# Attention and a sticky mixture of experts on one core: another written order for the same instructions

## The chip, the cores and the metric

The kernel runs on one core of a Trainium2 chip. The metric is device time in microseconds (us) of one execution, the median of several. The core has five instruction streams: TensorE (PE; its weight loads are listed as PEld), VectorE (DVE), ScalarE (ACT), GpSimd (POOL) and SyncE (SP), which here only issues DMAs. Each stream is worked off in the order in which the program issues it; streams wait for each other through semaphores.

## What is computed

First, causal attention with a decay on 8 batches of 8 heads, 576 positions and 64 values a head; its result, read as x of shape (8, 576, 512), goes through 8 experts. A position takes the expert of the position before it unless a local gate opens.

```python
scores = scale * q @ k.T + cum[:, None] - cum[None, :]      # cum = cumsum(log(clip(f)))
scores = where(causal, -1e9, scores); attn = softmax(scores)
x = (attn @ v)                                              # (B, S, H*D)
logits = x @ w_gate; local = sigmoid(x @ w_local)
for b, s:                                                   # in order of s
    fresh = argmax(logits[b, s])
    e = fresh if s == 0 or local[b, s] < 0.5 else prev_e
    out[b, s] = softmax(logits[b, s])[e] * (relu(x[b, s] @ w1[e]) @ w2[e])
```

## The kernel before

The program has two stages, one after the other: attention of all batches, up to about 369 us, and the experts, up to the end. Fp32 values are carried as pairs of fp16 numbers (a high and a low half), so a product is three matmuls.

**Attention.** A batch consists of 24 score units and a last one that needs no scores of its own. A unit runs through parts, each on one engine, and each part has a letter: S the scores on PE (L785, L792) into one of four PSUM banks `st`; M the maximum on DVE (L796) and N its joining (L890); E the exponential on ACT (L816); T four turns on PE (L830) into one of two banks `pt`; H the high half on ACT (L835); L the low half on DVE (L839), or in some units U on PE (L842) and K on ACT (L847) in its place; A the product with v on PE (L810). R and W divide (L861, L865 on DVE).

**What a batch needs.** q and k are loaded (L193, L197), split into halves by POOL (L317 to L327) into `t16q` and `t16k`, turned by DMA transposes from SP's queue (L362, into `Aq` and `Ak`; q and k are letters), and copied in part by further DMAs from the same queue into `QB` and `KB` (L370, L374; u and y). Scores read all four, in halves of four heads. `Aq` and `Ak` have two buffers each, `t16q` and `t16k` one. The result x is split by POOL (L317, L318), stored (L677), turned by DMA (L673 into `xt`, L701 into `xlt`; x and j) and multiplied with the gate's weights on PE (L735; g). Every second batch ends a group of tokens, for which steps of the routing follow (r): DVE finds the sticky choice, `G` (L1138 to L1148), PE turns it (L1153), and so on.

**What sets the order.** No scheduler: `ORDER` (L45) is a string of these letters, 2,244 of them, and `issue()` (L1042) walks it, issues the part that a letter names, for the oldest unit or step that has one left, and stops at the next S. `THEN` (L71) is a second string, of 314 letters, for the first part of the experts' stage: each letter asks one of 15 streams for its next piece (L1930), b products of early gathered tokens (L1809), c and d hidden values, e and f outputs (L1822), g the routing of the last group (L1901, L735, L1268 and on), h its probabilities, i the first expert's weights (L1620, L1607), j and k further weights, l and m gathered tokens, n ranks. So a letter's place in a string is the place of its instructions in the queues of the engines, SP's among them. z0 to z3 in `ORDER` (0, 1, 2, 3) are products of the first gathered tokens (L1533, hidden values L1539 and L1542) at attention's end.

Of the kernel before, what the change touches and what calls it, by code (L numbers as in the profile page):

```python
# [44 lines left out]
ORDER = (  # L45
    "SSMSMddMEddSTEMSHSdLTEMAHdSLTEMAHSMETLESHMSELTAEMSHMTSEMALHdSRELTWSHMTEALHSUREWTKMSHMdTEMAAHLtTEtLAcMHAcLRTSTW"
    "AHtEHUMEtKRtELTTcHAccttWHScUMALcSSETMMKEESTttHMHccAAyuuuULKANTSSERRTWWMbSMHNHLLE."
    "NAATTMHNHSLyLAAAEETTHbRbMSSWRbHWLSLbpETTMifiSAAAMHHLMTEEALAvMtHiSvELERMTTcHHLiLESfAWSMTiTiMASSHAHLLTpEEATHHMMx"
    "ASpUpElSKRELRWWTTMbMHLHEpSESATppyHMASSMEELTLAppAHTMEsAUSqpMHRWRUKKSqEpMbMTTHSHWAEELLAATTHSUMMHSKLEMpAEvRTTpHAH"
    "pNkUKuSsWRSLTTEAMMNHHWSE."  # L50
    "pNpLpATlLyHMASTEHAANSLxMpbTRREjSELpMbbTppHHWLEpfSMLEMpAASSTTHHkbbAMELWLAAiMETTygSSRWHHLLiiAAgEiiMMyuTuTfHHgLAL"
    "SSlTEEvTvMpAHiMSHlLSppRELAMTpEMTWRWpHSpHUKSEEpLATMAMxTxSSHEjAALEMMvTHHALSEERRWWTqUMgSgsKgSTpMppAHHLSLArEEMTTSr"
    "HHpUAMrLMEAuKrRETTrNpSpkrsrrHHAULETrMKWSTRNrEpWSHrMrAAAHLNMLEyTA."
    "HNRSrqLkppTEArppMHrbbTWSSLRTAHMLETMHbErLAHSSTLrTpEppWMHHrrbAAyLiLArMSpEfTTMRiiASrSirirHHuELLWbEMMTxTuHHAArrpES"
    "pSLTELbHTSMMALMpEvvAirTRRHySExHUSfKrlWSELTAHprWpMMAArSvsEETLTpMHHlpAAMSSLRRLMjrEpqTTESrSHWrLEprpTWMHHAALpEMMAk"
    "rUppAKSspTAMTuERHLHSWTLEESMTMppgggARHNSrpHyNLbbqWTLbkESTpEAHpMAAMNLrNEH."
    "ATLpHRESLpTTHHSSRWWLMMTALiiiEEfppMruAAAHSLTSApSHMEMLEETTAiiHbRHSSMWiELLTTMMfSSHHAyrALTrLEAErTlSMAMHpHrRLLMpEES"
    "THTpHSrUSRWAKTEHWrMLbrlrMLprErrrAESMrrbATxyrrMxpSrvHAjERETSrLMrHMqARrgrTUESHSKWLuTTggMMSEbrMHHruUvppAWEELrrppS"
    "KrrTpMSHMArTLAAENpHpksAyTLRETvrHHksRbWWSSApLNTAqLyrbMpTErHbMHNLAApN."
    "rpTEHSELrLprrubMRrfupTSTHHWArrLRALMESSErTHMMEEpTpWbvpLSiArTSSiiMMiiHHrrALLAATpEMTESSAHHrRLLrvWrsrTTfMMEHLHAALE"  # L60
    "EASSMrTTRMHESAErppLTRirHSvWUHMrLWrSKMMATAAlTAESpprHpEHLrTELpHMSTAsSyrRMEWRSHrpppLUrEWSTpbMMKTHHxxpLSAMMlApAEEk"
    "rrrTAUpqESKRHTLjSAHTMEMHULNKRSNWWMTppprTAyAHLHEAENEruSkArLqTT."
    "gpMrbbbrNHHrgEARLWLTpgArRHLTppSSTfrWrHMMrrLSSEHSLMMETTSEiAAApiipMrrHHMLLEASRTuuEHMiiTWHiLSLMrASrlETTASAAMEHHLp"
    "pELRTMETrrHAHWrrrySELvLSfvxTSHySMMRETEblLxMrWprAMHLESErSTpprrjbsHqMvMEASAATrHpLrMrTAHRRUSKLMSEETWpgMgHgSEMTUpp"
    "HKApprpSWETrpppALHTAArpHMpSkErLpNALTRETMWurSSHNRHrLELyW."
    "ArTrHMrTMAANrHNAUERKLErSTSrHWTHrMrEMSrELrLArkTSTrMAHsqAyrRLrSMrEHppAEASLTTHMMSWSrEEALMHRTiriLrSTEiAHHMurLELeeT"
    "HrMeeSMTEiiiWSSeeMLErelAAAMuTSeSsHHLURrMKrAWRTrMExHTWEAlAeeeerLHjrLSETSeerATHAEMLMHRALeTSsSxHTWeeAEErHUUKKyeeT"
    "TeRSSMrHHWAeeAMrLTEreLH01Mre2METAHLRrA3rRTEErWSeLWrrHUTKAAHMLNSMAhEATTHHeeRggNWzSLgLSMMNAeETEANER0123H00T1Wrhz"
    "2sH1r230L130LeThhTzzHHA1232L03e0hsh12e.13z2hALAA3zzRhWz"
)  # L70
# [2106 lines left out]
```

## Time and profile before

| | us |
|---|---|
| median of 3 runs | 768.9 (767.83 to 770.14) |
| the profiled execution | 768.85 |
| its span | 766.8 |
| PE busy | 716.1 (93%) |
| DVE, ACT, POOL busy | 478.0, 416.1, 409.9 |
| mean granted clock of TensorE | 0.985 |

The span is the stretch of the profiled execution between its first and last instruction; 2.05 us lie around it. Batches begin on PE at 15.4, 59.3, 95.8, 140.2, 180.2, 224.3, 269.9 and 310.2 us; the last score unit at 354.8. They are called batch 0 to 7.

### The profile page before, as it was taken

To read this page: it belongs to the slowest core of one execution; us is meant where nothing else is said; L and a number is where in the kernel's file an instruction comes from. 1 tells how busy PE (TensorE), PEld (TensorE's weight loads), DVE (VectorE), ACT (ScalarE), POOL (GpSimd) and SP (SyncE) were. 2 spreads that over 40 slices of the span, in tenths; PEclk is the share of its full clock that TensorE was granted. 3 is DMA by queue.
4 is the path that set the end of the run, shared out by engine and by line. 5 is a ranking of instruction groups with operands and counts; after the bars stand their busy time and mean duration, and the time that the engine had idled before them with its cause. 6 is when DMAs were issued, how large, how long until landed. Compare 5 with 4: busy or idle time off the path is not lost. (4 is left out here: it accounts for less than half of the span.)

```text
span 766.8 us, 20737 instructions
## 1 busy us (share of the span) xinstructions
PE 716.1 (93%) x8400; PEld 507.9 (66%) x8400; DVE 478.0 (62%) x1055; ACT 416.1 (54%) x795; POOL 409.9 (53%) x515
## 2 busy tenths in 40 slices
...
GB/s 197 224 160 234 199 229 207 215 204 235 202 219 283 185 228 199 211 231 110 204 265 105 257 40 230 148 231 81 185 180 90 240 103 198 175 125 167 44 7 46
DMA packets 181251, 136.07 MB, mean 177 GB/s; under 512 B 143971, under 2 KB 151397, under 8 KB 181111
## 3 DMA queue, kind: packets, MB, share of 16 engines
...
## 5 line engine op out<-in xcount | busy, mean ns | idle before, releaser
L816 ACT ACTIVATE P<-st,nm 128x512 f32<-128x512 f32 (+3 forms) x288 | 144.0, 561 | 14.5 <-DVE nm L890 7.5
L1442 PE MATMUL z<-xT,wh 128*128 128x300 f16 (+7 forms) x832 | 144.6, 289 | 0.3 <-DVE hl L1429 0.3
L796 DVE TENSOR_REDUCE nm<-st 128x1 f32<-128x512 f32 (+4 forms) x264 | 133.5, 542 | 9.5 <-PE st L792 6.9
L835 ACT CAST ph<-pt 128x512 f16<-128x512 f32 (+1 forms) x200 | 113.1, 587 | 36.9 <-PE pt L830 34.9
L830 PE MATMUL pt<-ident,P 128*128 128x128 f32 x784 | 117.7, 281 | 8.2 <-DVE pl L839 3.2
L839 DVE TENSOR_TENSOR pl<-pt,ph 128x512 f16<-128x512 f32 (+1 forms) x171 | 111.9, 667 | 11.9 <-ACT ph L835 11.1
L1434 POOL DMA_INDIRECT out_dram<-o,ranki x23 | 24.2, 1050 | 158.4 <-ACT o L1433 142.1
L1429 DVE SCALAR_TENSOR_TENSOR hl<-z,hh 128x240 f16<-128x240 f32 (+7 forms) x64 | 42.4, 662 | 96.2 <-ACT hh L1428 94.6
L1469 PE MATMUL y<-ul,hh 128*128 128x512 f16 (+2 forms) x440 | 101.1, 309 | 0.9 <-issue 0.9
L1469 PE MATMUL y<-uh,hh 128*128 128x512 f16 (+2 forms) x440 | 101.5, 311 | 0.1
L1469 PE MATMUL y<-uh,hl 128*128 128x512 f16 (+2 forms) x440 | 101.1, 309 | 0.1
L830 PEld LDWEIGHTS pt<-ident,P 128*128 128x128 f32 x784 | 84.6, 142 | 21.2 <-DVE pl L839 6.4
L1442 PEld LDWEIGHTS <-wh 128*128 128x128 f16 x832 | 80.8, 97 | 26.5 <-issue 0.7
L1442 PE MATMUL z<-xT,wl 128*128 128x300 f16 (+7 forms) x416 | 94.4, 289 | 0.0
L1469 PEld LDWEIGHTS <-hh 128*128 128x128 f16 (+2 forms) x880 | 56.9, 100 | 54.0 <-issue 6.1
L810 PE MATMUL xp<-VH,pl 128*128 128x65 f16 (+1 forms) x960 | 88.8, 195 | 2.6 <-DVE pl L839 2.3
L810 PE MATMUL xp<-VH,ph 128*128 128x65 f16 (+1 forms) x960 | 89.7, 196 | 0.0
L810 PE MATMUL xp<-VL,ph 128*128 128x65 f16 (+1 forms) x960 | 89.3, 195 | 0.3 <-issue 0.3
L810 PEld LDWEIGHTS <-ph 128*128 128x128 f16 (+1 forms) x1920 | 82.6, 103 | 7.5 <-issue 4.0
L1428 ACT ACTIVATE hh<-z 128x240 f16<-128x240 f32 (+7 forms) x64 | 36.7, 574 | 91.7 <-PE z L1442 88.3
L785 PE MATMUL st<-KB,QB 70*128 70x512 f16 (+5 forms) x384 | 77.2, 300 | 9.6 <-DMA KB<-Ak 6.9
L785 PE MATMUL st<-Ak,Aq 128*128 128x512 f16 (+5 forms) x384 | 77.1, 303 | 0.8 <-DVE nm L890 0.3
...
## 6 DMA issues: line engine op xcount, KB each, us to landing
...
```

Of the source, the lines that this page charges most:

```text
L785: nc.tensor.matmul(st[p0:p0 + m, co:co + n], lhsT=queries(lq, kk, h, c), rhs=rhs, start=(ps == 0 and first and co == col), stop=(ps == 1), ...
L796: nc.vector.tensor_reduce(dst, src, axis=AX.X, op=ALU.max, negate=True)
L810: nc.tensor.matmul(xo, lhsT=a[:, c0:c0 + m], rhs=w[:, vi, :], start=False, stop=(i == n - 1 and jj == 2), skip_group_check=True)
L816: nc.scalar.activation(P[:, c0:c1], st[:, c0:c1], AF.Exp, bias=bias)
L830: nc.tensor.matmul(U["pt"][:, i * 128:(i + 1) * 128], lhsT=P[:, i * 128:(i + 1) * 128], rhs=ident, is_transpose=True, start=(i == 0), stop ...
L835: nc.scalar.copy(U["ph"][:, :cols], U["pt"][:, :cols])
L839: nc.vector.tensor_tensor(U["pl"][:, :cols], U["pt"][:, :cols], U["ph"][:, :cols], ALU.subtract)
L1428: nc.scalar.activation(hv, z[:, 0:nh, 0:wd], AF.Relu)
L1429: nc.vector.scalar_tensor_tensor(lv, z[:, 0:nh, 0:wd], 0.0, hv, ALU.max, ALU.subtract)
L1434: nc.gpsimd.indirect_dma_start(out=outf, out_offset=bass.IndirectOffsetOnAxis(ap=scat(t), axis=0), in_=o, in_offset=None, bounds_check=NT ...
L1442: nc.tensor.matmul(z[:, a, 0:wd], lhsT=w[:, d, fc * 128:(fc + 1) * 128], rhs=xT[:, x, a * wd:(a + 1) * wd], start=(i == 0), stop=(i == len ...
L1469: nc.tensor.matmul(y[m * r:m * r + m, 0:w], lhsT=a[:, fc, c0:c0 + m], rhs=u[:, fc, w * r:w * r + w], start=(i == 0), stop=(i == len(prods) ...
```

## The change

Two string constants hold other permutations of the same letters; every letter occurs as often as before, and no function, buffer or shape differs. Lines keep their numbers. The diff is the two strings and nothing else; a line of each:

```diff
 ORDER = (
-    "SSMSMddMEddSTEMSHSdLTEMAHdSLTEMAHSMETLESHMSELTAEMSHMTSEMALHdSRELTWSHMTEALHSUREWTKMSHMdTEMAAHLtTEtLAcMHAcLRTSTW"
...
+    "SSMSMddMEddSTEMSHSdLTEMAHdSLTEMAHSMETLESHMSELTAEMSHMTSEMALHdSRELTWSHMTEALHSUREWTKMSHMdTEMAAHLtTEtLAcMHAcLRTAHt"
...
 THEN = (
-    "gggbbgbhhhbbbggbbbbbihbbgbbbcjgghjbbgbhhhhhgghbgbhhbhbbibbgdhjhbjjjbhhhiibhbbhbigbggbbggkkbbbbgghgjbbbbgebggbb"
...
+    "hggbbbbghbghhhhihhbbbbbhhhhgghbbbbhbgjhhhhgbbbjbbbbbbhghbbbggigbhgbbigbbiiggghbbbbjjgggebbkjcgbbgggbdbbbgbgcgg"
...
```

The first line of `ORDER` is the same up to its last few letters. Behind them the units' parts, the DMAs and POOL's splits interleave in another way, batch by batch. Three places follow.

**PE, end of batch 2**, where the first group's sticky choice `G` is turned (L1153). Before:

```order
L785 MATMUL st<-KB_122,QB_120 64x512
L785 LDWEIGHTS QB_120
L785 MATMUL st<-KB_122,QB_120 64x512
L1153 LDWEIGHTS kp
L1153 MATMUL st<-ident_72,kp 128x128
L1153 LDWEIGHTS G
L1153 MATMUL st<-ident_72,G 128x128
```

After:

```order
L785 LDWEIGHTS QB_120
L785 MATMUL st<-KB_122,QB_120 64x512
L842 LDWEIGHTS minus
L842 MATMUL pt<-ph,minus 128x512
L830 MATMUL pt<-ident,P 128x128 x4
L1153 LDWEIGHTS kp
L1153 MATMUL st<-ident_72,kp 128x128
L1153 LDWEIGHTS G
L1153 MATMUL st<-ident_72,G 128x128
```

A second set of scores (one more unit), a subtraction (L842) and four turns (L830) now stand between the step that makes `G` and its turn.

**SP, batch 5, the second half of its heads** (the forms with 128x20x128 are the turns of heads 4 to 7 and the last chunk; QB1 and KB1 are the buffers that this batch's scores read). Before:

```order
L362 DMA_TRANSPOSE Ak_5174<-t16k_5173 128x20x128
L677 DMA xs_60<-xr_4452 128x2x1024
L193 DMA ldq_5151<-in_q_dram 128x1024
L362 DMA_TRANSPOSE Aq_4502<-t16q_4501 128x20x128
L370 DMA KB1_123<-Ak_5174 64x2048
L197 DMA ldq_5151<-in_q_dram 128x256
L193 DMA ldk_5421<-in_k_dram 128x1024
L370 DMA QB1_121<-Aq_4502 64x2048
L193 DMA ldk_5421<-in_k_dram 128x1024
L374 DMA QB1_121<-Aq_4502 64x512
```

After:

```order
L362 DMA_TRANSPOSE Aq_4305<-t16q_4304 128x20x128
L677 DMA xs_60<-xr_4407 128x2x1024
L193 DMA ldk_5433<-in_k_dram 128x1024
L370 DMA QB1_121<-Aq_4305 64x2048
L374 DMA QB1_121<-Aq_4305 64x512
L343 DMA QB0_120<-augm_61 3x4096
L352 DMA QB0_120<-augt_62 3x512
L362 DMA_TRANSPOSE Ak_4796<-t16k_4795 128x20x128
L193 DMA ldk_5433<-in_k_dram 128x1024
L197 DMA ldk_5433<-in_k_dram 128x256
L370 DMA KB1_123<-Ak_4796 64x2048
```

The two turns changed places, and both of q's copies now stand between them; k's copy comes last.

**POOL, attention's end** (x of batch 7 is split by L317 and L318; L1407 gathers tokens; L1381, L324 and L327 prepare weights; L696 clears `xlt` ahead of its last multiplication with the gate's weights). Before:

```order
L317 TENSOR_SCALAR xr<-xn 128x2x512
L318 TENSOR_TENSOR xr<-xn,xr 128x2x512
L317 TENSOR_SCALAR xr<-xn 128x512
L318 TENSOR_TENSOR xr<-xn,xr 128x512
L1381 TENSOR_SCALAR stg<-stg 128x1024
L1407 DMA xg<-xs,xg 128x1024 x4
L324 TENSOR_SCALAR uh<-stg 128x1024
L327 TENSOR_TENSOR ul<-stg,uh 128x512 x2
L696 MEMSET xlt 128x64
```

After:

```order
L317 TENSOR_SCALAR xr<-xn 128x2x512
L318 TENSOR_TENSOR xr<-xn,xr 128x2x512
L317 TENSOR_SCALAR xr<-xn 128x512
L318 TENSOR_TENSOR xr<-xn,xr 128x512
L1407 DMA xg<-xs,xg 128x1024 x4
L1381 TENSOR_SCALAR stg<-stg 128x1024
L324 TENSOR_SCALAR uh<-stg 128x1024
L327 TENSOR_TENSOR ul<-stg,uh 128x512 x2
L696 MEMSET xlt 128x64
```

The weights' scaling (L1381) went from ahead of the four gathers to behind them. On PE, the turn of the last x (L1901) was followed at once by the gate's multiplication (L735); now sixteen matmuls of the early products (L1809) stand between them, and four groups of three matmuls of L1533, before one, stand ahead of L1901 behind attention's last A.

## Rows read from the trace of the kernel before

**Rows 1.** Windows: start:end length, busy us (instructions) by engine, granted clock, DMA share, GB/s.
```profile
60.00:400.00 340.00, 310.98 (x5053) 249.39 (x5050) 299.55 (x729) 254.30 (x542) 265.80 (x304) 0.97 0.96 215
...
360.00:400.00 40.00, 33.45 (x378) 24.23 (x377) 25.89 (x67) 11.24 (x22) 18.97 (x17) 0.87 0.81 234
400.00:766.00 366.00, 358.20 (x2772) 223.50 (x2770) 131.35 (x237) 116.07 (x166) 87.94 (x121) 1.00 0.51 140
```
The engines' columns are PE, PEld, DVE, ACT, POOL, in this order.

**Rows 2.** Windows of the three stretches at half clock.
```profile
133.40:140.20 6.80, 6.80 (x70) 4.65 (x69) 4.26 (x13) 3.61 (x8) 6.46 (x7) 0.50 0.89 190
...
198.20:201.60 3.40, 3.40 (x28) 3.02 (x27) 2.40 (x8) 0.44 (x1) 1.13 (x1) 0.50 1.24 135
...
372.30:382.50 10.20, 7.73 (x103) 7.64 (x100) 3.77 (x24) 1.06 (x4) 4.17 (x5) 0.50 0.70 170
```
**Rows 3.** Waits of PE: line, what for; us in total, times, longest us.
```profile
PE st L785 <- DMA KB<-Ak: 6.9, 4, 2.1
...
PE st L785 <- DMA QB<-Aq: 2.7, 2, 1.7
PE st L1153 <- DVE G L1148: 2.6, 2, 1.7
...
PE xp L810 <- DVE pl L839: 2.3, 4, 1.0
```
**Rows 4.** Timeline of PE: start, duration; in brackets the wait before it.
```profile
198.02 0.42 PE L785 MATMUL st<-KB,QB 70*128 70x512 f16 x1 [2.11 <-DMA KB<-Ak]
...
225.77 0.38 PE L785 MATMUL st<-KB,QB 70*128 70x512 f16 x1 [1.06 <-DMA KB<-Ak]
...
243.14 0.39 PE L785 MATMUL st<-KB,QB 70*128 70x512 f16 x1 [1.72 <-DMA QB<-Aq]
...
285.26 0.38 PE L785 MATMUL st<-KB,QB 70*128 70x512 f16 x1 [2.10 <-DMA KB<-Ak]
```
**Rows 5.** Timeline of SP's queue, batch 5: start, time to issue.
```profile
223.75 3.68 SPq L362 DMA_TRANSPOSE Ak<-t16k  x1
...
228.62 5.35 SPq L362 DMA_TRANSPOSE Aq<-t16q  x1
...
237.48 0.47 SPq L370 DMA_DIRECT2D QB<-Aq  x1
...
238.62 0.92 SPq L374 DMA_DIRECT2D QB<-Aq  x1
```
**Rows 6.** Timeline of SP's queue, ahead of batch 2.
```profile
90.33 3.94 SPq L673 DMA_TRANSPOSE xt<-xr  x1
```
**Rows 7.** `G`: timeline of DVE and POOL; then all four of L1148, ns min/median/max.
```profile
130.92 1.32 DVE L1148 TENSOR_TENSOR G<-G,F 128x10 f16<-128x10 f16 x1
...
129.46 2.75 POOL L327 TENSOR_TENSOR t16k<-ldk,t16k 128x640 f16<-128x640 f32 x2
...
L1148 DVE TENSOR_TENSOR G<-G,F x4: 161/613/1320, 130.9 to 380.0; 128x10 f16<-128x10 f16 x4
```
**Rows 8.** Timeline of PE at attention's end.
```profile
370.95 0.38 PE L1901 MATMUL psG<-ident,xl 128*128 128x128 f16 x4 [1.69 <-DVE hl L1542]
372.12 0.57 PE L735 MATMUL psG<-wg,xt 128*128 128x18 f16 x16 [0.78 <-DVE xlt L1905]
...
376.62 0.20 PE L735 MATMUL psG<-wg,xlt 128*128 128x18 f16 x1 [2.47 <-POOL xlt L696]
...
384.31 0.22 PE L1809 MATMUL z<-xT,wl 128*128 128x128 f16 x1
384.36 0.38 PE L1822 MATMUL y<-uh,hh 128*128 128x512 f16 x1
```
**Rows 9.** Timeline of POOL and SP at attention's end.
```profile
358.29 1.05 POOL L1381 TENSOR_SCALAR stg<-stg 128x1024 f32<-128x1024 f32 x1
360.93 1.05 POOL L1407 DMA_INDIRECT xg<-xs,xg  x1 [1.59 <-DVE xs L1347]
...
379.24 1.14 SPq L1620 DMA_DIRECT2D stg<-in_moe_w_dram  x2
```

More of the change, by code (lines that the diff above doesn't have):

```diff
@@ L45 @@
 ORDER = (
-    "SSMSMddMEddSTEMSHSdLTEMAHdSLTEMAHSMETLESHMSELTAEMSHMTSEMALHdSRELTWSHMTEALHSUREWTKMSHMdTEMAAHLtTEtLAcMHAcLRTSTW"
[L47 to L67, printed above, removed]
@@ L68 @@
-    "TeRSSMrHHWAeeAMrLTEreLH01Mre2METAHLRrA3rRTEErWSeLWrrHUTKAAHMLNSMAhEATTHHeeRggNWzSLgLSMMNAeETEANER0123H00T1Wrhz"
-    "2sH1r230L130LeThhTzzHHA1232L03e0hsh12e.13z2hALAA3zzRhWz"
+    "SSMSMddMEddSTEMSHSdLTEMAHdSLTEMAHSMETLESHMSELTAEMSHMTSEMALHdSRELTWSHMTEALHSUREWTKMSHMdTEMAAHLtTEtLAcMHAcLRTAHt"
+    "RWTcUEEWHSKttLMtTTcccStHHEAUScSLMTKAMTEEStHHMMAEucAANtEUKSSRcTRWLWuuyMTSAAMb."
+    "HHNbNLLTESHMTELNAAHTbbMLSREAHfTSSWyLRHMTELMWHviAiiipALTEHESiSTLMMTSAAAbMHLHELEEtTTScHHMSLSRLifWppMMMpbAEETASHT"
@@ new lines @@
+    "HLLEESAAMTxTRApppyHHSUWSLMRMKTTESpWHAHALAELTTAEsxHHMAllUqvpREUKRKqMESSppMMWpTTHLWSSAEHETMpHEALSUTAAbMMKTSpHRWH"
+    "ULEATvEkSSsHMNKRATWLETMMuHSNHyE."
+    "LLAAMTHSpNALNRbjAkEEWTSHTHpSMELbgTfpLTSAMMApppRbHbppbWLHAAppLEEMAiSTSgyTgMfEHHMvSuiuESLLiiRiEippTHMxAWTSSLHlpE"
+    "LAyTTMvlAMxHpSpHLAAEETLTHHMMSSRLMsUTEWRSEAKWTjSpEHMMSLqHMEAALEATHSEsTpgHSRUWMMppgLgrrMpuETASpKrrTkHARpEvLbEHTW"
+    "rHMSSrEULAyKTMATrMSHHAbLAETNSpMEpRRppHSNLEpUppKWMM."
+    "WTHbqNNrATrLSArHLTEbMHAAALrrREpTRrWEWiHTiiLfrHSSTHSSMELLTHMAEAMLTSMrrTHkEAAiSbMALiiHEEppTLHTrrRSMpHLLpfpWSArTT"
@@ new lines @@
+    "EHHuuMAMASErllyLxALvxMRsrSbvMTTSEHHLAUEEpRrSTpWMMSrKAHpLjWESTETMHHqMAAAryrsLLrSTTEMEAHSpppppkRSpburHLLTpTyERSH"
+    "rWMMSHEvEWAUAMMrpLKqESrbTrTMHHrNApppAkELLSbrMEbTARRHNTWLSS."
+    "uHpWLMEATSTMfNHppLMHppNAEApEARyLATWSTSREMHHWgLrTAAELggMTiiiHHELiiLSMSTpMTHHLExEAAATLrrHSTySvLSfSHRMbMiETWLlAxA"
+    "ATbApplpjpHSpMMEHELLEMrSTTAHHbSRRrErLrrSWuWUKSTpppTMrMAAAHErHELLgTrTgAMrgrrrHErrSrqrrSrSrMrLMMTHEUESSEKMrRMpAp"
+    "EHTMHrvWLSrTksAEvMHrRESrWUruSLryMrApKTTArpNMbAHHAEErLLRNRTHbWWSTS."
+    "EMSLTqNppAppMApHEHrSLsNbfELTTAHpAAMMHrrLLSpRRTTrruWEHEuppkprLSMMATHLAApSrHLTTEEWSbbririiSHHMfELLAArTATSMHHrSEM"
```

13 lines of the change are left out of this document (11 added, 2 removed).

## The prediction, made blind

> **What bounds the kernel now.** I read the windows first. From 60 to 400 us, TensorE is busy 310.98 of 340 us; from 400 to 766 it is busy 358.20 of 366 [rows 1]. The reader is to see two different stages: behind 400 us the experts keep TensorE full, and an order of the same instructions has 7.8 us of gaps to work on, spread thin; between 60 and 400 lie 29.0 us of gaps, 6.55 of them in the last 40 us. The same row shows why: DVE is busy 88% there and the share of the DMA engines is 0.96, so TensorE's suppliers are almost as full as TensorE itself. Next come the stretches at half clock: 6.80, 3.40 and 10.20 us at a granted clock of 0.50 [rows 2], which is the lower level, 1.2 GHz, where everything else runs at 2.4. At full speed the PE work in them (6.80, 3.40, 7.73) would take half as long; the clock costs up to 9.0 us. Each began a little behind a long wait of TensorE: for `G` before 133, for `KB` at 198, for the last x and the gate at 371 to 372 [rows 4, 8]. A long wait isn't always followed by one: those at 243 and 285 were not [rows 4]. Then the waits themselves: for the copies of k 6.9 us in 4, of q 2.7 in 2, for `G` 2.6 in 2, for the low half ahead of the product with v 2.3 in 4 [rows 3]. These are what another order can take away or add to.
>
> Nothing is removed and nothing added, so each term below is a wait that goes, comes or moves. The sum is made against the profiled execution, 768.85 us, of which 766.8 are the span; the median of the runs shown is 768.9, so a saving is read off directly. About 0.3% (2.3 us) is what a measurement of this kernel can tell from no change.
>
> **Routing.** Of the waits for `G` one is the longest, 1.7; the other is the rest of 2.6, 0.9 [rows 3]. Before, nothing stands on PE between the scores that DVE handles ahead of `G` and the turn of `G`. After, a second set of scores, a subtraction and four turns stand there. The last products of 128 columns start 0.05 us apart [rows 8], so a matmul of 512 columns counts 0.2: four for the scores and one for the subtraction 1.0, the fp32 turns, each taken as four fp16 matmuls, 0.8. With what else the order moved behind the scores that DVE waits for, I count 3.5 us; the bare three parts are 1.8. That covers 1.7. In the third group the same count goes from 1.2 to 3.4 us, so its 0.9 goes too. In the second group it falls from 0.8 to 0; there a new wait can arise between 0 and 1.7; I take 0.9, the value of the milder of the two waits seen. Sum: -1.7 - 0.9 + 0.9 = **-1.7 us**, between -2.6 and -0.9.
>
> Why `G` is late can be read: L1148 works on ten elements a partition and took 1.32 us, while its shortest of four took 0.161; POOL was in two subtractions (2.75 us together, from 129.46), and the second of these ends at 132.21, as L1148 does at 132.24 [rows 7]. The Trainium skill, page "SBUF — State Buffer", section "SBUF: two separate sides", says that a VectorE operation with two SBUF inputs and a GpSimd operation that reads SBUF exclude each other, the later one waiting for the whole instruction. The trace agrees at this place, to 0.03 us. By that rule the wait depends on where POOL's subtractions fall, not on PE's row alone: the second group, which loses its cover, would wait the full 1.7 if a subtraction falls there, and the term would be -0.9 where I take -1.7.
>
> **The copies for the scores.** The waits that may move: 2.11, 1.06, 1.72, 2.10 [rows 4] and 0.96 (the rest of the 2.7 for q [rows 3]); 7.95 together.
> - Batch 5, second half (1.72 before). From the start of its first turn to the end of the last copy before: 223.75 to 239.54, 15.8 us [rows 5]. Aq's turn ended at 233.97 and the copy from it went at 237.48: 3.5 us of landing. Now q's turn comes first with its two copies, then k's turn, then k's copy: 5.35 + 3.5 + 0.47 + 0.92 + 3.68 + 3.5 + 0.6 (a copy) = 18.0. That is 2.2 later, so the wait becomes 3.9, if the chain does not begin earlier.
> - Batch 5, first half (1.06): POOL's splits for it stand 4.4 us of POOL's work further forward; it goes.
> - Batch 2, first half (none before): the turn of x that stood behind k's copy, 3.94 us [rows 6], now stands ahead of q's turn and both copies. Between 0 and 3.9; SP had pauses there and the copy went well ahead of its scores, so I take 1.0.
> - Batch 2, second half (0.96): two small puts more ahead of it, 1.5. Batch 4 (2.11): the same SP work ahead as before, 2.1. Batch 6 (2.10): 1.7 us less of SP work ahead, 0.4.
>
> Sum after: 3.9 + 0 + 1.0 + 1.5 + 2.1 + 0.4 = 8.9, against 7.95: **+1.0 us**, between -3 (batch 5's chain begins with the earlier splits) and +4.
>
> **Attention's end.** The named waits: 1.69, 0.78 and 2.47 [rows 8]. The first is in truth for the last x: division, split and turn follow the last product with v. Three matmuls of L1533 covered it, now twelve do, of 256 columns (0.11 us each, half of one with 512): 1.0 more cover, 0.7 left. The second is covered by sixteen matmuls of the early products that now stand between; 0.05 us apart at full clock [rows 8], 0.9 in all, so 0. The third is for POOL's clearing of `xlt`, which stands behind the gathers. The weights' scaling of 1.05, which ended 1.6 us ahead of the first gather [rows 9], is now behind the gathers, so this alone gives the gathers nothing; but the indices for them (the wait of 1.59 for DVE [rows 9]) stand one unit earlier on DVE, and x's split one unit earlier on POOL. I count the gathers some 3.5 us earlier, the clearing some 2.5 to 3 earlier with the 1.05 now ahead of it, and the wait as gone. Together 4.94 - 0.7 = 4.2 saved. Not all of it is kept: right behind, at 384.36, the outputs need the weights whose load SP issued at 379.24 [rows 8, 9]; this load stands behind the turns of the gathered tokens, and so moves with them, about 3.5. I take **-3.5 us**, between -1 and -4.9.
>
> **Distances inside the units.** With the new interleaving, the low half is issued directly ahead of its product in 9 places and not in 17; of the 2.3 us that such waits cost [rows 3] I take half back. Against it, scores that reuse a bank just freed by the exponential stand close behind it in 26 places and not in 14; no large wait of this kind is in the trace, so 0 to 2, and I take 0.5. Sum **-0.6 us**.
>
> **The clock.** The stretch of 6.80 at 133.4 follows the wait for `G`, which goes: its PE work at full speed gives back 3.4. The new wait of 3.9 in batch 5 may bring one such stretch; three of the five long waits in the rows did, so half of 3.4 (1.7) is put against it, and 0.8 for the other new ones, a quarter of 3.4. The one at 198 stays, the one at 372 I leave. Sum **-0.9 us**, between -9.0 (all gone) and +7 (two more stretches like the longest behind a wait in the batches).
>
> **The sum.** -1.7 + 1.0 - 3.5 - 0.6 - 0.9 = -5.7: 768.85 - 5.7 = **763.1 us**. Behind 400 us I cost the new order of `THEN` at nothing: the products there are full and the gathered tokens arrive before the work ahead of them is done; if that cover is gone, a turn of some 4 us more shows.
>
> **Rivals.**
> 1. *No net change, 768.2 us.* The suppliers set the pace: DVE at 88% and DMA at 0.96 between 60 and 400 [rows 1] deliver the same things in another order, so a gap that closes reopens at the next copy, and the end's gain is lost in the loads behind it. For it: the size of the DMA waits in every later batch. Against it: gaps at the end and at `G` are not supplied by DMA. Only the distances inside the units remain, -0.6: 768.2. The Trainium skill, page "Perfetto Trace Analysis", section "What "DMA-bound" means", counts an issuing engine's sequencer that is solid with DMA slices as such a bound; SP's queue in batch 5 has such a row of turns, but also pauses, as that at 237 [rows 5], so here the rule holds in part.
> 2. *Slower by SP's queue, 772.5 us.* The copies in batch 2 and 5 come late as counted or worse (+1.0 and +2 more, the upper part of batch 2's bound), each wait brings a half-clock stretch of which 3.4 is lost (+6.8 against the -3.4 regained at 133), and the end gives only 1.5 for lack of weights: with the distances at +0.4, -1.7 + 3.0 - 1.5 + 3.4 + 0.4 = +3.6, 772.5. It decides when batch 5's last copy starts more than 2 us behind the scores that ask for it.
> 3. *Slower by the gate of batch 6, 771.6 us.* Two turns of x (3.94 each by [rows 6]) and one of its low half now stand shortly ahead of the multiplication with the gate's weights, with 6 us of PE work in between where 12 to 18 were. If they land late, TensorE stalls up to 5 us there and falls to half clock (3.4): -5.7 + 5 + 3.4 = +2.7, 771.6.
> 4. *Much faster, 756 us.* All waits as in the sum, and the stretches at 133 and 372 don't come: -1.7 + 1.0 - 4.2 - 0.6 - 3.4 - 3.9 (half of 7.73) = -12.8, 756.0.
>
> **How the numbers follow.** The forecast 0.39; rival 1 0.22; rival 2 0.16; rival 3 0.10; rival 4 0.13. Faster by over 0.3% (under 766.6) are the forecast and rival 4, 0.52; within, rival 1, 0.22; slower (over 771.2) rivals 2 and 3, 0.26. The range leaves out the far half of the slower cases and of rival 4: 756.5 to 773.5. The likeliest case has a range of its own, 760 to 766.5.
>
> **What would show it.** Right: no wait above 0.3 us at the first and third L1153; no half clock near 133; waits at L1901, L735 and behind it under 1.5 us together; the first L1822 about 3.5 us nearer to the end of the last score unit. A wait of 3 to 4 us for `KB` in batch 5's second half and none in its first. Wrong: a wait for `xt` or `xlt` at the gate of batch 6; a half-clock stretch behind a copy in batch 2, 5 or 6; a start of the first fixed expert (L1442) that is not earlier although attention ends earlier.

## The result and the profile after

The changed kernel takes 758.9 us (median of four runs, 757.56 to 760.79) against 769.5 for the kernel before in the same session: a ratio of 0.9865 with a 95% interval of 0.9831 to 0.9898, so 10.6 us faster by the medians. Run again in another session it took 760.96 against 769.83, a ratio of 0.9888 (0.9858 to 0.9918). The forecast was 763.1 and the range 756.5 to 773.5: the direction and the range held, the gain was about one and a half to two times as large as forecast (8.9 and 10.6 us by the medians, where 5.7 was forecast). The profiled execution of the changed kernel took 757.93 us, its span 755.9.

The windows of the changed kernel, with the columns of [rows 1], and its three stretches at half clock, which answer to [rows 2]:

```profile
60.00:400.00 340.00, 313.98 (x5086) 249.93 (x5085) 307.52 (x743) 253.88 (x542) 264.70 (x305) 0.98 0.96 216
122.40:125.80 3.40, 3.40 (x27) 2.71 (x25) 1.97 (x9) 2.57 (x7) 1.45 (x2) 0.50 1.08 279
177.00:180.40 3.40, 3.10 (x39) 2.79 (x40) 0.86 (x3) 1.47 (x4) 2.56 (x5) 0.50 1.01 189
368.20:371.60 3.40, 3.32 (x63) 3.16 (x61) 3.08 (x17) 0.41 (x3) 0.97 (x2) 0.50 1.12 148
360.00:400.00 40.00, 35.84 (x380) 23.54 (x378) 30.55 (x73) 11.05 (x22) 17.00 (x16) 0.96 0.69 194
```

The time at half clock is 10.2 us in three stretches where it was 20.4. Each of them again lies beside a long wait: for the turned low half of x (`xlt`) ahead of 122, for the copy `KB` at 177, for the turn of the last x at 367. The waits of TensorE, in the columns of [rows 3]:

```profile
PE st L785 <- DMA KB<-Ak: 7.3, 5, 3.8
PE pt L830 <- DVE pl L839: 5.3, 8, 1.6
PE psG L1901 <- DVE hl L1542: 2.4, 1, 2.4
PE st L785 <- DMA QB<-Aq: 1.8, 2, 0.9
PE st L735 <- DMA xlt<-xl: 1.6, 1, 1.6
PE xp L810 <- DVE pl L839: 1.6, 2, 1.3
```

The waits for `G` are gone. The waits for the copies are not: 7.3 and 1.8 where 6.9 and 2.7 stood [rows 3]. They stand at other places. Timeline of TensorE: a new wait at the gate's multiplication in batch 2, the first turn of `G`, the longest wait for a copy, and attention's end (which answers to [rows 8]):

```profile
122.01 0.36 PE L735 MATMUL st<-wg,xlt 128*128 128x18 f16 x8 [1.62 <-DMA xlt<-xl]
...
134.36 0.22 PE L1153 MATMUL st<-ident,G 128*128 128x128 f16 x1
...
177.30 0.58 PE L785 MATMUL st<-KB,QB 70*128 70x512 f16 x1 [3.77 <-DMA KB<-Ak]
...
367.19 0.38 PE L1901 MATMUL psG<-ident,xl 128*128 128x128 f16 x4 [2.39 <-DVE hl L1542]
368.71 0.58 PE L735 MATMUL psG<-wg,xt 128*128 128x18 f16 x16
...
369.99 0.36 PE L735 MATMUL psG<-wg,xlt 128*128 128x18 f16 x8
...
375.71 0.38 PE L1822 MATMUL y<-uh,hh 128*128 128x512 f16 x1
```

The first output (L1822) starts 8.65 us earlier than before, 22.3 us behind the last score unit instead of 29.6; some 2 of these 7.3 us are only that less of TensorE's work stands between the two in the new order. Behind 400 us the two kernels go alike, except that the profile before has two pauses of TensorE of about 1 us each in an output (L1469; 0.44 us of each are shown as a wait, put down to "issue") which the changed one lacks. Those come and go: of the later profiles in the old order some have none, and one in the new order has both. They are no part of the change, and 2 of the 10.9 us between the two profiled spans are theirs.

**Where along the program.** The two profiles alone can mislead, since an execution of this kernel varies by some 2 to 3 us (standard deviation of a run). So I put the time against the work: every matmul counts with the usual distance to the next one of its line and shape at full clock, and two executions are compared at the same amount of work. The table takes four profiles whose batches stand in the old order (from 345 us on: six with the old end) and five in the new (from there on: seven with the new end), the experiments below among them. It gives mean times of a stretch, and what of the difference was idle time of TensorE and what was loss at half clock; the rest is gaps too short to be shown as waits. The stretches are named by the times of the profile before. Their bounds are not sharp, since the two orders put different matmuls beside them: with a slightly different usual distance the last four rows come out as -0.4, -0.2, -2.8 and +0.3 us.

| stretch, us | old, us | new, us | difference | idle | half clock |
|---|---|---|---|---|---|
| 9 to 86 | 76.9 | 75.6 | -1.3 | -0.4 | 0 |
| 86 to 141 | 54.3 | 53.9 | -0.4 | +0.8 | -2.1 |
| 141 to 166 | 24.9 | 23.5 | -1.4 | -1.1 | +0.2 |
| 166 to 194 | 30.1 | 33.0 | +2.8 | +2.5 | +0.9 |
| 194 to 221 | 26.5 | 26.1 | -0.4 | 0 | -0.8 |
| 221 to 278 | 55.1 | 52.8 | -2.3 | -1.9 | +0.3 |
| 278 to 301 | 24.2 | 22.7 | -1.5 | -0.1 | -0.4 |
| 301 to 345 | 44.1 | 45.1 | +0.9 | -0.5 | -0.1 |
| 345 to 402 | 57.0 | 53.5 | -3.5 | -0.8 | -1.5 |
| 402 to 759 | 356.8 | 356.8 | 0 | +0.2 | 0 |

Three things are to be seen. What the first batches win by 166 us (3.1 us) is nearly all spent again by 194, in the wait for batch 4's copies. Batches 5 and 6 (221 to 301 us) win 2.8 to 3.8. The end wins 2.8 to 3.5. All rows together are about -7, less than the medians of the runs differ by: each row stands on a handful of executions.

The granted clock is known for every run. (1 - clock) times the span is the time that the lower clock can have cost; it includes the program's end, where TensorE has stopped. The means of this cost are 12.3 and 10.6 us for the kernel before (34 and 28 runs of two sessions), and 8.3 us for the changed one (6 runs of the second). One run of before in each session was over 1.5% slower than the fastest and is left out here. So the clock is 2.2 us of the change by means in one session (95% interval 0.9 to 3.5), not the 5.1 of a comparison of the two profiles' half-clock stretches.

### The profile page after: what moved, and what is told of

Same layout as the page of the kernel before. It is cut to its first block, busy times and chain, and to the rows that moved or that the text cites. A ratio compares the mean times of both kernels' runs of the same rounds, so it can differ in the third digit from the quotient of the medians.

```text
span 755.9 us, 20716 instructions
## 1 busy us (share of the span) xinstructions
PE 709.2 (94%) x8400; PEld 503.8 (67%) x8400; DVE 480.9 (64%) x1055; ACT 415.0 (55%) x795; POOL 404.7 (54%) x515
## 5 line engine op out<-in xcount | busy, mean ns | idle before, releaser
L1442 PE MATMUL z<-xT,wh 128*128 128x300 f16 (+7 forms) x832 | 144.6, 289 | 0.3 <-DVE hl L1429 0.3
L830 PE MATMUL pt<-ident,P 128*128 128x128 f32 x784 | 117.7, 280 | 8.2 <-DVE pl L839 5.3
L1469 PE MATMUL y<-uh,hh 128*128 128x512 f16 (+2 forms) x440 | 101.0, 310 | 0.0
L1469 PE MATMUL y<-uh,hl 128*128 128x512 f16 (+2 forms) x440 | 100.7, 309 | 0.0
L1469 PE MATMUL y<-ul,hh 128*128 128x512 f16 (+2 forms) x440 | 100.7, 309 | 0.0
L1442 PEld LDWEIGHTS <-wh 128*128 128x128 f16 x832 | 80.9, 97 | 26.5 <-issue 0.7
L830 PEld LDWEIGHTS pt<-ident,P 128*128 128x128 f32 x784 | 84.2, 142 | 20.2 <-DVE pl L839 7.1
L1442 PE MATMUL z<-xT,wl 128*128 128x300 f16 (+7 forms) x416 | 94.4, 289 | 0.0
L1469 PEld LDWEIGHTS <-hh 128*128 128x128 f16 (+2 forms) x880 | 56.7, 100 | 53.1 <-issue 5.2
L810 PE MATMUL xp<-VH,pl 128*128 128x65 f16 (+1 forms) x960 | 87.1, 194 | 1.6 <-DVE pl L839 1.6
L810 PE MATMUL xp<-VH,ph 128*128 128x65 f16 (+1 forms) x960 | 87.6, 195 | 0.0
L810 PE MATMUL xp<-VL,ph 128*128 128x65 f16 (+1 forms) x960 | 87.4, 195 | 0.0
```

Of the source, the lines that this page charges most:

```text
L810: nc.tensor.matmul(xo, lhsT=a[:, c0:c0 + m], rhs=w[:, vi, :], start=False, stop=(i == n - 1 and jj == 2), skip_group_check=True)
L830: nc.tensor.matmul(U["pt"][:, i * 128:(i + 1) * 128], lhsT=P[:, i * 128:(i + 1) * 128], rhs=ident, is_transpose=True, start=(i == 0), stop ...
L1442: nc.tensor.matmul(z[:, a, 0:wd], lhsT=w[:, d, fc * 128:(fc + 1) * 128], rhs=xT[:, x, a * wd:(a + 1) * wd], start=(i == 0), stop=(i == len ...
L1469: nc.tensor.matmul(y[m * r:m * r + m, 0:w], lhsT=a[:, fc, c0:c0 + m], rhs=u[:, fc, w * r:w * r + w], start=(i == 0), stop=(i == len(prods) ...
```

## The experiments

Kernels of one session share its runs of the kernel before, and ratios are to those; sessions differ by some us, so ratios and not times are compared between them.

### The two strings apart

order_alone has the new `ORDER` and the old `THEN`, then_alone the reverse.

```diff
 # order_alone
 ORDER = (
-    "AHtEHUMEtKRtELTTcHAccttWHScUMALcSSETMMKEESTttHMHccAAyuuuULKANTSSERRTWWMbSMHNHLLE."
+    "RWTcUEEWHSKttLMtTTcccStHHEAUScSLMTKAMTEEStHHMMAEucAANtEUKSSRcTRWLWuuyMTSAAMb."
...
 # then_alone
 THEN = (
-    "gggbbgbhhhbbbggbbbbbihbbgbbbcjgghjbbgbhhhhhgghbgbhhbhbbibbgdhjhbjjjbhhhiibhbbhbigbggbbggkkbbbbgghgjbbbbgebggbb"
+    "hggbbbbghbghhhhihhbbbbbhhhhgghbbbbhbgjhhhhgbbbjbbbbbbhghbbbggigbhgbbigbbiiggghbbbbjjgggebbkjcgbbgggbdbbbgbgcgg"
...
```

> The new ORDER with the old THEN. The full change gave 758.9 us against 769.5, -10.6. Theory A (gains add up along the program: about -5.5 in batches 0 to 6, the rest at attention's end, and little that the order of THEN does by itself): -7 to -9 us, the half-clock stretches at 133 and 198 gone and the one at 372 either shortened or as before (10 us). Theory B (the end's gain comes from THEN, which fills TensorE behind the turn of the last x): -5 to -6 us and the stretch at 372 still 10 us long.

Measured: 764.04 us, ratio 0.9911 (0.9878 to 0.9944), -6.9 us. The time from the last score unit to the first output is 22.7 us in its profile, as with the whole change (22.3), though its `THEN` is the old one. The waits at the end tell the two strings apart. Timeline of TensorE of order_alone:

```profile
371.56 0.20 PE L735 MATMUL psG<-wg,xt 128*128 128x18 f16 x2 [0.78 <-DVE xlt L1905]
...
373.55 0.19 PE L735 MATMUL psG<-wg,xlt 128*128 128x18 f16 x1 [0.42 <-POOL xlt L696]
```

The wait for the cleared `xlt`, 2.47 before, is 0.42 already; that is the new `ORDER`, which lets the gathers start sooner. The 0.78 is unchanged; that is the wait that only the new `THEN` covers. The gain lies just short of what theory A expected, and its half-clock stretches did not go but stand at 138, 179, 309 and 374 us, 3.4 us each.

> The old ORDER with the new THEN. Theory A: -1 to -2.5 us, the waits of 0.78 (first gate product) and part of the 2.47 (cleared xlt) covered by the sixteen early products, the batches as before with both half-clock stretches at 133 and 198. Theory B: -4 to -5 us, with the half-clock stretch at 372 down from 10.2 to about 3.4 us.

Measured: 771.40 us, ratio 1.0004 (0.9965 to 1.0043). The new `THEN` by itself gives nothing that can be measured (the interval is -2.7 to +3.3 us, so theory A's -1 to -2.5 is not excluded). Theory B is out: the end's gain comes with the last batch's letters in `ORDER`.

### The batches and the end apart

Each takes a beginning of one order and then what is left over in the other's order. all_but_end: new in batches 0 to 6. end_alone: old in batches 0 to 6, then new, with the new `THEN`. The cut is behind the full stop that ends batch 6 (the rest of both strings is left out here):

```diff
 # all_but_end: the new lines up to the full stop, what is left of the old ones behind
     "UWAHrKEMrMApvrpppqLrkSuAAAMRErWTTRsHrSppHLLpTrEEHMLTrrHNSASpELTTMHWNUMyHAArpLAErqSKrNRrTpM."
-    "rENWARHSSELTTMppkMHHLSEEpAppLSrTMMHWTrSiLrAHAAASMRTEELHTWyrMLESSHrMAAiuTiEMrESSEiLSrTeHHeeMSMLAiTEAMHLeirRTLrH"
+    "pppNEESSHWTHMrEMSrELrLArkTSTrMAHAyrRLrSMrEHppAEASLTTHMMSWSrEEALMHRTiriLrSTEiAHHMurLELeeTHrMeeSMTEiiiWSSeeMLEre"
...
```

> The new order in batches 0 to 6, then what is left in the old order (batch 7, attention's end, the old THEN). Theory A: the gain of the batches arrives: -4 to -6.5 us. Rival (the suppliers set the pace and a closed gap reopens later): within 2 us of the old time, with the gain lost in the waits for copies of batch 7 or for weights behind attention's end.

Measured: 767.67 us, ratio 0.9968 (0.9934 to 1.0002), -2.5 us. Short of the 4 us that theory A expected at least, above the 2 us of the rival, and not clear of nothing.

> The old order in batches 0 to 6, then what is left in the new order (batch 7, attention's end, the new THEN). Theory A: -3.5 to -5.5 us, with first outputs (L1822) about 22 to 24 us behind the last score unit instead of 29.6, and together with the batches' part the full -10.6 within 2 us. Rival (not additive): nearly all of -10 us, or nothing.

Measured: 767.54 us, ratio 0.9955 (0.9922 to 0.9989), -3.5 us; the first output comes 23.7 us behind the last score unit. The mean cost of the lower clock is 8.2 us against 12.3 for the kernel before in the same session: by means the whole gain of the end is the clock (-4.1 us, with an interval of 1.4 us to either side). The two parts add to -6, where the whole was -8.9 and -10.6; but each part is known to some 2.6 us only, so it isn't shown that anything is missing. The seams of these hybrids also have waits of their own.

### The wait for `G`

rows_later moves the turn of `G` in the kernel before behind a product, a subtraction and four turns, about what the change does there:

```diff
-    "HHpUAMrLMEAuKrRETTrNpSpkrsrrHHAULETrMKWSTRNrEpWSHrMrAAAHLNMLEyTA."
+    "HHpUAMrLMEAuKrRETTrNpSpkrsrHHAULETrrMKWSTRNrEpWSHrMrAAAHLNMLEyTA."
```

> The kernel before with one letter moved: the first turn of the sticky choice (L1153) stands behind one more product, subtraction and set of four turns on TensorE (about 1.8 us). Theory A: the wait of 1.73 us at 132 goes and with it the half-clock stretch of 6.8 us: -3 to -5 us there, of which the copies of k later take some back: -2 to -4 us at the end. Rival (the suppliers set the pace): the gain is all given back at the next wait for a copy, -1 to 0 us.

Measured: 770.09 us, ratio 1.0038 (1.0005 to 1.0071): no gain, if anything slower. Its timeline and windows of TensorE (lines are one higher than in the other kernels) say why:

```profile
135.19 0.33 PE L831 MATMUL pt<-ident,P 128*128 128x128 f32 x1 [1.80 <-DVE pl L840]
```
```profile
135.70:142.50 6.80, 6.80 (x68) 4.58 (x66) 4.09 (x13) 3.80 (x9) 6.44 (x7) 0.50 1.08 200
```

The wait for `G` is gone, and 1.80 us of waiting for DVE's low half stand 3 us further on, with the same 6.8 us at half clock behind. DVE's two steps of `G` end when POOL's subtractions end [rows 7]; in rows_later `G` is done at 134.53 us and the subtraction at 134.51. So all that is queued behind them on DVE is late, and what TensorE does in between only decides which result it misses first.

filled leaves the order of before and has TensorE repeat a matmul 31 times in that wait (for the first group only), so that it works while it waits:

```diff
-            for i, x in enumerate((kpw, gw)):
-                nc.tensor.matmul(ps[:, 128 * i:128 * i + 128], lhsT=x, rhs=ident16, start=(i == 0), stop=True,
+            for i, x in enumerate((kpw,) * (32 if g == 0 else 1) + (gw,)):
+                nc.tensor.matmul(ps[:, 128 * (x is gw):128 * (x is gw) + 128], lhsT=x, rhs=ident16, start=x is kpw, stop=True,
```

> The kernel before, with the wait of 1.73 us for the sticky choice filled: TensorE repeats a matmul of the row ahead of it 31 more times (128 columns, about 0.05 us each, the same result), so that it waits as long but works meanwhile. Theory A (the pause lowers the clock): the half-clock stretch at 133 goes, and mean half-clock time falls by 3 to 7 us; time -1 to -3 us. Rival (the stretch doesn't come from this pause): half-clock time as before, 24 to 25 us, time within 1 us or slower.

Measured: 771.46 us, ratio 1.0025 (0.9997 to 1.0052). In its profile the stretch behind is at full clock (timeline, then the window that was half clock before):

```profile
130.37 1.96 PE L1154 MATMUL st<-ident,kp 128*128 128x128 f16 x32
```
```profile
132.40:140.20 7.80, 7.47 (x117) 5.66 (x118) 7.77 (x21) 5.92 (x13) 7.48 (x9) 1.00 1.02 191
```

That agrees with the pause as the cause of that stretch, in one execution. It is weak evidence: of the four profiles that keep this wait of 1.7 us (before, end_alone, last_but_one, then_alone) one has 6.8 us at half clock behind it, two have 3.4, and one has none. And over twelve runs the mean cost of the lower clock did not fall: 12.5 us, against 10.6 for the kernel before in that session. Stretches at half clock came elsewhere. So taking one pause away does not save its stretch in the mean; why not stays open.

### Batch 4's copies

The wait of 3.77 at 177 is the largest in the changed kernel. SP's queue ahead of it, in the changed kernel:

```profile
161.93 2.35 SPq L362 DMA_TRANSPOSE Aq<-t16q  x1
...
166.73 2.85 SPq L362 DMA_TRANSPOSE Ak<-t16k  x1
...
172.77 0.47 SPq L370 DMA_DIRECT2D KB<-Ak  x1
```

x_later moves a turn of x and that of its low half from ahead of these turns to behind all four of batch 4:

```diff
-    "EHHuuMAMASErllyLxALvxMRsrSbvMTTSEHHLAUEEpRrSTpWMMSrKAHpLjWESTETMHHqMAAAryrsLLrSTTEMEAHSpppppkRSpburHLLTpTyERSH"
-    "rWMMSHEvEWAUAMMrpLKqESrbTrTMHHrNApppAkELLSbrMEbTARRHNTWLSS."
+    "EHHuuMAMASErllyLxALvMRsrSbvMTTSEHHLAUEEpRrSTpWMMSrKAHpLWESTETMHHqMAAAryrsLLrSTTEMEAHSpppppkRSpburHLLTpTyERSHrW"
+    "MMSHEvEWAUAMMrpLKqESrbTrTMHHrNApppAkxjELLSbrMEbTARRHNTWLSS."
```

> The changed kernel with one turn of x of batch 3 and the turn and puts of its low half (about 7.7 us of SP's queue) moved from ahead of batch 4's q and k turns to behind all four of them. Theory A (SP's queue is the chain behind the wait of 3.77 us for k's copy at batch 4): that wait falls under 1 us, the half-clock stretch behind it goes, and the kernel is 3 to 5 us faster than the changed one, 754 to 756. Rival (the suppliers' total sets the pace): the wait moves to a later copy or to the gate of batch 3, and the time stays within 2 us of the changed kernel's.

Measured: 763.01 us, ratio 0.9927 (0.9902 to 0.9952), where the changed kernel had 0.9888 beside it: not faster than that, if anything slower. Timeline of TensorE of x_later:

```profile
172.51 0.38 PE L785 MATMUL st<-KB,QB 70*128 70x512 f16 x1 [1.15 <-DMA KB<-Ak]
...
183.12 0.25 PE L735 MATMUL st<-wg,xt 128*128 128x18 f16 x3 [5.84 <-DMA xt<-xr]
```

The wait for the copy fell to 1.15, nearly to the 1 us of theory A, and a wait 2 us larger came at the gate, as the rival had it.

j_later moves only the turn of the low half, into the pause in which SP waits for k's turn to land:

```diff
-    "EHHuuMAMASErllyLxALvxMRsrSbvMTTSEHHLAUEEpRrSTpWMMSrKAHpLjWESTETMHHqMAAAryrsLLrSTTEMEAHSpppppkRSpburHLLTpTyERSH"
+    "EHHuuMAMASErllyLxALvxMRsrSbvMTTSEHHLAUEEpRrSTpWMMSrKAHpLWESTETMHHqMAAAryrsLLrSTTEMEAHSpppppkjRSpburHLLTpTyERSH"
```

> The changed kernel with one letter moved: the turn and the puts of the low half of batch 3's x (3.5 us of SP's queue) stand behind k's turn for batch 4, in the pause in which SP waits for that turn to land, and no longer ahead of q's and k's turn. Theory C (this chain is what TensorE waits 3.8 us for): k's copy is issued 1.5 to 3 us earlier, the wait falls to 1 to 2 us, and the kernel is 1.5 to 3 us faster than the changed one. Rival (the DMA engines, not the queue, set the time of that copy): its issue is earlier, its landing not, and the wait and the time stay.

Measured: 760.06 us in another session, ratio 0.9922 (0.9900 to 0.9944): no gain over the changed kernel. SP's queue and TensorE in j_later:

```profile
158.79 4.80 SPq L362 DMA_TRANSPOSE Aq<-t16q  x1
...
165.92 2.83 SPq L362 DMA_TRANSPOSE Ak<-t16k  x1
...
173.11 0.54 SPq L370 DMA_DIRECT2D KB<-Ak  x1
...
178.86 0.38 PE L785 MATMUL st<-KB,QB 70*128 70x512 f16 x1 [4.62 <-DMA KB<-Ak]
```

q's turn starts 3.1 us sooner and takes 2.5 us longer to issue, so k's turn starts only 0.8 sooner, and the copy is issued no earlier at all. The DMA engines' mean share between 60 and 400 us is 0.96 in the changed kernel; room in the queue isn't what this copy lacks. Neither theory C nor the rival holds as written, since both expected an earlier issue. The result speaks for the rival's cause: the transfers ahead, not the place in the queue, set when that copy goes. It doesn't show it. Of two places tried, one moved the wait and one left it.

### Which batches the gain comes from

first_three has the new order in batches 0 to 2, last_but_one in batches 4 to 6, all else old. They are cut at ends of batches as above: behind a cut stands what the letters ahead of it have left over. The lines with the cuts (the rest is left out):

```diff
 # first_three: new up to the full stop, what is left of the old order behind
+    "WrHMSSrEULAyKTMATrMSHHAbLAETNSpMEpRRppHSNLEpUppKWMM.rTrTrWHrrAAAHLNLETAHNRSrqLkTEArMHrTWSSLRTA"
...
 # last_but_one: old up to the first full stop, then new, from the second one on old
+    "krUppAKSspTAMTuERHLHSWTLEESMTMppgggARHNSrpHyNLbbqWTLbkESTpEAHpMAAMNLrNEH.buSfppMpppERyLATWSTSR"
...
+    ".pppNEESSHWTHMrEMSrELrLArkTSTrMAHAyrRLrSMrEHppAEASLTTHMMSWSrEEALMHRTiriLrSTEiAHHMurLELeeTHrMee"
...
```

> The new order in batches 0 to 2, all else in the old order. In every profile of the new order so far the lead that these batches win (3 to 5 us at 166 us) is spent again by 194 us, in the wait for batch 4's copies. Theory C (the copies' chain sets the time there, so the lead of the first batches is worth nothing): within 1.5 us of the kernel before. Theory A (the gains add up): -3 to -4.5 us.

Measured: 764.93 us, ratio 0.9980 (0.9955 to 1.0006), -1.6 us and not clear of nothing. The lead of 4.2 us that its profile has at 166 us is 2.2 by 278 us. That is nearer to theory C than to A's -3, which the interval does not exclude; by the means little of the first batches' gain survives.

> The new order in batches 4 to 6, all else old. Theory C (what remains of the change is won where the copies no longer wait: batch 5's waits of 1.06 and 1.72 us gone, 2 to 3.5 us between 221 and 278 us): -2.5 to -4 us, TensorE's idle time in that stretch of work down from 5.7 to about 2.3 us. Prediction's step (batch 5 waits longer by the exchanged turns): +1 to +2 us, a wait of 3 to 4 us for KB in its second half.

Measured: 769.28 us, ratio 1.0042 (1.0021 to 1.0063): slower. In the stretch that theory C spoke of it was right: 221 to 278 us take 3.6 us less, idle time 2.7 where 5.7 was. But the seam to the old order ahead brings a wait at the gate, and more half clock:

```profile
207.88 0.20 PE L735 MATMUL st<-wg,xt 128*128 128x18 f16 x1 [3.00 <-DMA xt<-xr]
```

The mean cost of the lower clock is 13.6 us against 11.0 for the kernel before, 2.6 more, where the kernel is 2.8 us slower. A stretch that wins 3.6 us does not make a kernel that wins them.

### The exchanged turns of batch 5

turns_back puts batch 5's second half back: k's turn first, q's copies last.

```diff
-    "EMSLTqNppAppMApHEHrSLsNbfELTTAHpAAMMHrrLLSpRRTTrruWEHEuppkprLSMMATHLAApSrHLTTEEWSbbririiSHHMfELLAArTATSMHHrSEM"
-    "LRETHLWprTMALSHMAErALppTlAyiiEMvHrSRLTSTiRHUMppEHMWvpKrWSSTAALEEMHMLSxqMTAAEvrrrHRrrTyLrEHESSTpUWHSMrKSEMTASpp"
+    "EMSLTkNppAppMApHEHrSLsNbqfELTTAHpAAMMHrrLLSpRRTTrryWEHEppuprLSMMATHLAApSrHLTTEEWSbbririiSHHMfELLAArTATSMHHrSEM"
+    "LRETHLWprTMALSHMAErALppTlAuiiEMvHrSRLTSTiRHUMppEHMWvpKrWSSTAALEEMHMLSxqMTAAEvrrrHRrrTyLrEHESSTpUWHSMrKSEMTASpp"
```

> The changed kernel with the turns of batch 5's second half and their copies put back into the old order (k's turn first, q's copies last). Theory C (the exchange is not what matters, the chain simply begins earlier): no wait for a copy there, within 1.5 us of the changed kernel. Rival (the exchange is what removed the wait): a wait of 1 to 2 us for QB there and 1 to 3 us slower than the changed kernel. Prediction's step (the exchange costs 2.2 us of the chain): no wait either, since none is left to save.

Measured: 763.51 us, ratio 0.9958 (0.9932 to 0.9985), against 0.9922 for j_later beside it, which has the new turns: 3.4 us slower than that by the medians. In its profile the stretch from 221 to 278 is back to 57.6 us (before 56.2, changed 52.6). So the exchange matters, as the rival said, but not by the wait that the rival named: no wait for a copy is there. What waits is POOL, then DVE, then TensorE. Timeline of turns_back, SP's queue, POOL, DVE and TensorE:

```profile
219.22 5.31 SPq L362 DMA_TRANSPOSE Aq<-t16q  x1
...
227.93 0.47 SPq L370 DMA_DIRECT2D QB<-Aq  x1
...
228.15 1.05 POOL L324 TENSOR_SCALAR t16q<-ldq 128x1024 f16<-128x1024 f32 x1 [7.24 <-ACT ldq L378]
...
242.83 0.56 DVE L865 TENSOR_TENSOR xn<-xp,rs 128x384 f32<-128x384 f32 x1 [5.81 <-POOL xr L327]
...
243.44 0.16 PE L800 MATMUL xp<-eps 128*128 128x2 bf16 x1 [5.04 <-DVE xn L865]
```

The same split of POOL, the first of batch 6's q, in the changed kernel and in the kernel before:

```profile
224.90 1.04 POOL L324 TENSOR_SCALAR t16q<-ldq 128x1024 f16<-128x1024 f32 x1 [0.92 <-ACT P L816]
```
```profile
237.61 1.05 POOL L324 TENSOR_SCALAR t16q<-ldq 128x1024 f16<-128x1024 f32 x1 [0.66 <-DMA Aq<-t16q]
```

In all three it starts 0.1 to 0.2 us behind the issue of the copy QB, which waits for q's turn to land (224.79, 227.93 and 237.48 [rows 5]). `t16q` has one buffer: POOL can't split the next batch's q before the turn has read this one's. Put last, q's turn holds POOL up (7.24 us idle), POOL's splits of x come late, and DVE and TensorE wait for those. The profile names ACT in the bracket of turns_back, where the second half of q was scaled (L378) from 226.73 to 228.01 us. That is not the cause: in the changed kernel the same split begins at 224.90, 5 us ahead of the same scaling at 229.93. The agreement of the three starts with the turn's landing speaks for the buffer. That the buffer is the cause is read from three traces and one undone exchange; a second buffer was not tried. In the kernel before the same order cost POOL only 0.66 us, since its other work filled the time: what the exchange is worth holds for the new order around it.

### The whole once more

after_again is the changed kernel itself, without an edit.

> The changed kernel once more, beside the next three on one chip. All theories: about -10.5 us against the kernel before. By its clock over twelve runs it tells how much of this is TensorE's clock: by the two profiles alone 7.4 us of it (20.4 us at half clock before, 10.2 after), by the means of the earlier runs (24.7 us at half clock before, 16.3 in four runs after, the end of the program among it) 4.2 us.

Measured: 760.96 us, ratio 0.9888 (0.9858 to 0.9918), in six runs; the clock's share as given above, 2.2 us, below both numbers of the expectation (its 7.4 was no right sum: half of the 10.2 us less at half clock is 5.1).

## Why the prediction was right, and where not

**The sum.** Forecast -5.7, measured -8.9 and -10.6. The sign and the range came from a sum whose terms did not all hold.

**Routing, -1.7: the waits went as read, the time did not.** No wait is left at any L1153, 2.6 us less where 1.7 was forecast. But the stretch 86 to 141 us differs by 0.4 us, and its idle time rose by 0.8. In the changed kernel the cover is ample: the step that makes `G` is done at 129.68 us (timeline of DVE), and TensorE turns it at 134.36.

```profile
129.23 0.45 DVE L1148 TENSOR_TENSOR G<-G,F 128x10 f16<-128x10 f16 x1
```

What failed is that I put nothing on the gate in batch 2. There TensorE now waits 1.62 us for the turn of x's low half (122.01, above): it asks for it 2.5 us earlier than before, at 120.39 instead of 122.89, and SP issues the turn 1.45 us earlier, at 117.02 instead of 118.47. All eight profiles with the new order in batches 1 and 2 have this wait, 0.9 to 1.8 us long; none of the six with the old order has it. So a copy was late there, and not the routing.

rows_later shows a second gap in the count. I counted TensorE's work between two of its instructions, where in the old order the late engine was DVE, held up by POOL. The sentence in the prediction on what excludes DVE from its operands pointed there: by the Trainium skill (page "SBUF — State Buffer", section "SBUF: two separate sides") a VectorE operation with two SBUF inputs waits for the whole of a GpSimd operation that reads SBUF and started before it. The traces agree: `G` ends 0.02 us behind a subtraction of POOL in rows_later, and so it does in the changed kernel (129.68 and 129.66), where it began later into one and took 0.45 us instead of 1.32. The count was also too high: I put four fp32 turns at 0.8 us, and in the trace of the kernel before they start 0.109 us apart, 0.44 for four.

**Copies, +1.0: the total about right, by errors that cancel.** Behind batch 0 the waits for copies add up to 8.07 us, where 7.95 stood and 8.9 were forecast. At the places that I had priced they are 2.24 us, and 5.83 us stand at three that I had not: batch 4's first half (3.77), batch 7's first half (1.43) and later scores of batch 3 (0.63). Batch 5's second half was to wait 3.9 and waits nothing. Two steps failed. First, the chain of batch 5 was to be 18.0 us long; it is 16.0 from the first turn's start to the last copy's end, mainly because k's copy followed its turn by 1.9 us and not by 3.5, and q's turn took 4.16 us and not 5.35:

```profile
216.95 4.16 SPq L362 DMA_TRANSPOSE Aq<-t16q  x1
...
224.79 0.47 SPq L370 DMA_DIRECT2D QB<-Aq  x1
...
226.98 3.59 SPq L362 DMA_TRANSPOSE Ak<-t16k  x1
...
232.51 0.47 SPq L370 DMA_DIRECT2D KB<-Ak  x1
```

It also begins 6.8 us earlier [rows 5], where TensorE's batch begins 5.3 us earlier. Second, and larger, I put the exchange of the turns down as a cost of 2.2 us, by when the copies go out; turns_back shows it as a gain of about 3 us in the new order, most likely by when q's single buffer comes free. I had that fact in hand (one buffer of `t16q`) and followed the exchange only forward, to the scores, not back to POOL.

**Attention's end, -3.5: right in size, in part by luck.** The stretch from 345 to 402 us is 2.8 to 3.5 us shorter. Of the named waits 4.94 became 2.39: the second and the third are gone as forecast, the third by the earlier gathers, the second by the sixteen products. The first was to fall to 0.7 and grew to 2.39. I had it wait for the last x alone. In the changed kernel x's split is done at 365.81 us, and the turn starts at 367.19, 0.05 us behind the last of four steps L1542 that stand behind the split on DVE; before, one stood there. The split itself now meets the weights' scaling that moved behind the gathers on POOL (timeline of the changed kernel):

```profile
364.61 1.20 DVE L315 TENSOR_TENSOR xl<-xnl,xl 128x256 f16<-128x256 f32 x1 [0.47 <-ACT xl L314]
365.74 1.40 DVE L1542 SCALAR_TENSOR_TENSOR hl<-st,hh 128x256 f16<-128x256 f32 x4
```
```profile
364.50 1.04 POOL L1381 TENSOR_SCALAR stg<-stg 128x1024 f32<-128x1024 f32 x1
```

It took 1.20 us where it took 0.42 before. Two waits that I did not list came beside it: 1.04 us at 353.41, for L1542, and 1.51 at 384.82, for L1176. So the idle time of the stretch fell by 0.8 us only (table), where I had counted 4.2 us of waits. The rest is the clock and short gaps: the stretch at half clock behind these waits was 10.2 us and is 3.4, and the clock is 1.5 us of the end's gain by the table and all of it by the runs of end_alone.

**Distances, -0.6: the wrong sign.** The waits for the low half ahead of the product fell from 2.3 to 1.6, where I had counted half of them. Those ahead of the turns rose from 3.2 to 5.3; I had left them out.

**The clock, -0.9: mis-sized.** -2.2 us by the means of one session, -5.1 by the loss within the two profiles. The rule of the rivals, a stretch for each long wait, does not hold run by run (the profiles named at filled).

**Not counted.** 1.3 us in the first 86 and 1.4 from 141 to 166 us are made of small gaps and waits that I did not cost.

**The rivals.** "No net change" named what happens at the gate in batch 2 and at batch 4, where the first batches' lead is spent on the copies; it failed behind that, since batches 5 and 6 do win. The gate of batch 6 does not wait. "Much faster", 756.0, lies nearer to 758.9 than the forecast does (by the second session's -8.9 the forecast is the nearer one), but not by its reason: the stretches at half clock got shorter and moved, they did not go.

**The signs.** No wait at L1153, no half clock near 133 and an earlier start of L1442 (426.3 instead of 435.3) came as named; order_alone, though, has a half-clock stretch at 138. Missed: the waits at the end were to be under 1.5 us and are 2.39, the wait in batch 5 never came, and a half-clock stretch stands behind a copy in batch 2 (122.4).
